# A hand-planned attention and FFN kernel on one core: the first FFN's gates freed from Wu in the plan, GpSimd's sums booked on the shared port, a longer lead for instruction loads, and the whole order planned anew

## The chip, the cores and the metric

One core of a Trainium2 chip. The metric is device time in microseconds (us) of one execution. The engines are called as the profile calls them: PE (TensorE, matrix products), PEld (its weight loads), ACT (ScalarE), DVE (VectorE), POOL (GpSimd), SP (SyncE, which here only issues DMAs).

## What is computed

Four layers over one sequence of 2048 rows of 512 bf16 values: attention with a memory, FFN, and both again with the same weights. Cut to what matters:

```python
x = x + A(layernorm(x));  x = x + B(layernorm(x))
x = x + A(layernorm(x));  x = x + B(layernorm(x))

def A(x):                       # 32 heads of 16; 4 segments of 512 rows
    for s in range(4):
        p = softmax(qs @ ks.T * 16**-0.5 + causal mask)
        a_dot = p @ vs
        a_mem = (phi(qs) @ M) / (phi(qs) @ z + 1e-6)   # phi(t) = t + 1 if t > 0 else exp(t)
        o = g * a_mem + (1 - g) * a_dot                # g = sigmoid(beta), one per head
        M = M + phi(ks).T @ vs;  z = z + phi(ks).sum()
    return o @ wo

def B(x):
    return (gelu(x @ w_gate) * (x @ w_up)) @ w_down    # 512 -> 1792 -> 512
```

## The kernel before, in words

The two attention layers have four segments each, so there are eight segments k = 0 to 7 of 512 rows, each with its attention `Att(k)` and its FFN `Ffn(k)`. For one segment: layer norm of four row tiles (VectorE's statistics, then xn, L920), transposed into xnT by DMA or by PE; q, k, v by products of 128x512; 36 rounds of scores, taken in pairs, whose exponentials ScalarE writes into `pt` (L1864); masks on `pt` by GpSimd (L1813, L1818) or VectorE (L1823); "flushes", which multiply `pt` with the values; transposes back on VectorE (L1391, L1414), and, for segments with a memory, the sum of both attentions into `aT` (L1417) on VectorE or GpSimd. Then come `wo` (added to x, L1463), the norm for the FFN, 14 gate tiles and 14 up tiles (wg_sb, wu_sb), gelu on ScalarE, their product on VectorE (L1557), and four down tiles of 14 products each (wd_sb). The update of the memory is a chain on VectorE: macc (L1303), zacc (L1305; L1301 in a first segment), mblk (L1286), zcols (L1292).

Nothing of the order is written down line by line. `order` is a list scheduler that runs when the kernel is built: it keeps a clock for each engine (`Clocks`, `Engine`), books each operation with a fixed duration, and emits instructions in the order that its clocks give. Each engine then runs its own list in order, and the semaphores that the tiles require hold it where data or a buffer isn't there yet. So the planner's durations and conditions decide only the order and, for some operations, the engine; the chip's waits come from the data.

What the change touches in it:

- `POLICY` and `STAGES`: some 60 constants (due times, slacks, preferences between engines), a set for each 20 us of planned time.
- `Clocks.issue`: a model of how PE's instructions come in, in chunks of 256. At place 178 of a chunk the planner notes that the next one is asked for; at place `CHUNK_END` it lets PE stand until `FETCH` us after that.
- [...] In `Engine.serve` a job with a `Port` waits in the plan until the other engine's port is free, less 0.2 us; `Port(t, True)` is the soft kind, beside which the other engine only pays 0.15 us.
- `on_dve_or_pool` posts a job to both engines, and the one that comes to it first takes it; `pol.at_pool` moves GpSimd's claim on the sums of `aT` earlier or later.
- The weights are loaded by SP (L600): 4 pieces of Wo, 8 of Wg, 8 of Wu in the list `pieces`, 7 of Wd in `late_pieces`, each with a planned time. The times of the first three are `w_at + 1.2 kt` and `w_at + 5 + w_gap n`, n = 0 to 7 for Wg and 8 to 15 for Wu. When the last of `pieces` is posted, the event ("loaded", "first") is set at the planner's estimate of its landing plus 2.0 us.
- `gate`: a gate of any FFN may be planned once its xnT is there and `free()` holds, which asks for ("loaded", "first"). `early` lets a gate begin with half of xnT. `up` asks only for its gelu.
- If PE would find nothing to do while scores remain, the planner gives it a filler product from the tile `warm`.

Nearly all products go through one helper line, L541, so the profile tells them apart by their tiles: "ps<-xnT,wg_sb" is a gate. Four products of 32 columns or rows of PE stand for one whole product; PE is then in its "columns" or "rows" mode, and the planner books 0.109 us for each change of mode.

Of the kernel before, what the change touches and what calls it, by code (L numbers as in the profile page):

```python
# [37 lines left out]
CHUNK, CHUNK_ASKED, CHUNK_END, FETCH = 256, 178, 222, 3.7  # L38
# [27 lines left out]
def table(halved):  # L66
# [17 lines left out]
    if halved:  # L84
# [31 lines left out]
    rs_pool=32.757, f_urge=-233.244, quick=2, paired=8, turn_pe=1, turn_last=0, w_at=29.345, w_gap=2.17,  # L116
    wd_at=78.552, wd_gap=2.776, flush_wait=-13.887, piece_slack=40.254, kb_slack=24.368, mem_slack=-20.134,
    margin=0.5, qk_due=0.962, e_q=49.408, e_k=2.993, exp_slack=-6.401, e_slack=131.01, phi_slack=22.785,
    gelu_slack=-0.789, act_evict=1.671, first_evict=0.248, gate_step=93.832, up_due=-100.529, up_step=84.355,
    down_due=-29.196, down_step=-47.297, upd_due=91.807, kb_act=82.777, vz_slack=55.93, x_dve=2.467, v0_due=-11.641,  # L120
    x1_at=-87.497, x2_at=16.051, x3_at=24.107, x3_load=-378.834, direct=2, gelu_tiles=0, look=3, lag=0.852,
    wv_at=-320.502, xn_pool=19.822, kb_pool=121.576, cut_pool=154.009, at_pool=-238.466, pe_turns=0, gate_due=4.191,
    shun=8.799, col_gap=0.807, hold=5, early=104.615, starve=0.16, near=114.234, cap=13, soon=28.208, columns=0,
    kd_slack=-5.85, zero_slack=-1.031, hold1=-49.923, hold2=2.205, hold3=11.541, hold_step=-162.485, hold_v=23.995,
    park=3)
# [3 lines left out]
        rs_pool=0.722, quick=9, kb_slack=2.193, mem_slack=-24.231, e_q=-2.643, gelu_slack=-0.49, gate_step=79.021,  # L129
        up_due=-101.483, up_step=41.973, down_step=-58.4, upd_due=91.729, vz_slack=33.291, direct=8, gelu_tiles=2,  # L130
        lag=0.412, at_pool=-237.424, early=83.209, starve=60.426, soon=7.146, park=4)),
    (2, 3, dict(
        rs_pool=2.667, quick=6, turn_pe=0, kb_slack=55.298, mem_slack=-32.756, e_q=-2.851, gelu_slack=-0.49,
        gate_step=78.038, up_due=-98.977, up_step=25.491, down_step=-53.827, upd_due=91.729, vz_slack=14.093,
        x_dve=7.459, direct=6, gelu_tiles=2, look=2.764, lag=0.475, xn_pool=30.206, cut_pool=102.189,
        at_pool=-237.424, gate_due=8.415, starve=1.292, soon=7.146, park=5)),
    (3, 4, dict(
        rs_pool=4.794, turn_pe=12, kb_slack=51.509, mem_slack=58.674, e_q=50.036, e_k=1.445, gelu_slack=1.935,
        gate_step=78.038, up_due=-96.513, up_step=85.14, down_step=-56.495, vz_slack=40.138, x_dve=6.187, direct=6,
        look=2.618, xn_pool=30.206, cut_pool=118.125, at_pool=-208.534, gate_due=14.291, shun=21.0, early=101.394,  # L140
        starve=0.321, soon=7.146, park=2)),
    (4, 5, dict(
        rs_pool=-2.341, quick=0, turn_pe=12, kb_slack=85.554, mem_slack=58.674, qk_due=1.009, e_q=50.137, e_k=1.464,
        gelu_slack=0.429, gate_step=79.294, up_due=-96.513, up_step=84.505, down_step=-72.139, vz_slack=51.333,
        x_dve=6.187, direct=3, gelu_tiles=2, xn_pool=20.238, cut_pool=148.746, at_pool=-208.534, gate_due=8.415,
        shun=21.0, early=101.394, starve=0.453, soon=7.146, park=2)),
    (5, 6, dict(
        rs_pool=36.794, quick=0, turn_pe=12, kb_slack=66.017, mem_slack=58.674, qk_due=1.009, e_q=55.15, e_k=2.984,
        gelu_slack=-0.805, gate_step=79.294, up_due=-96.513, down_step=-70.89, vz_slack=18.865, x_dve=7.455,
        gelu_tiles=2, look=2.835, lag=0.71, xn_pool=20.238, cut_pool=148.746, at_pool=-208.534, gate_due=0.276,  # L150
        shun=21.488, soon=7.146)),
    (6, 7, dict(
        rs_pool=11.417, f_urge=-261.392, quick=0, paired=11, turn_pe=0, flush_wait=0.581, piece_slack=36.524,
        kb_slack=76.591, mem_slack=-10.427, qk_due=-0.609, e_q=97.288, e_k=-5.757, exp_slack=-18.942, e_slack=69.536,
        phi_slack=30.587, gelu_slack=0.965, act_evict=1.166, gate_step=33.55, up_due=-80.509, down_due=-55.61,
        down_step=-81.567, upd_due=143.06, kb_act=60.08, vz_slack=4.039, x_dve=18.331, direct=0, gelu_tiles=2,
        look=2.622, lag=0.754, xn_pool=-3.088, kb_pool=116.679, cut_pool=153.155, at_pool=-189.709, gate_due=0.226,
        shun=85.539, hold=8, early=169.131, starve=0.31, near=101.522, cap=11, soon=0.694, kd_slack=37.99, park=6)),
    (7, 8, dict(
        rs_pool=-52.581, f_urge=-61.761, quick=3, paired=0, turn_pe=13, flush_wait=-3.039, piece_slack=92.516,  # L160
        kb_slack=220.906, mem_slack=57.517, qk_due=-30.647, e_q=-54.782, e_k=89.983, exp_slack=-17.861,
        e_slack=55.594, phi_slack=96.482, gelu_slack=214.751, act_evict=-149.173, gate_step=5.34, up_due=-0.69,
        up_step=3.923, down_due=12.354, down_step=-3.42, upd_due=-3.412, kb_act=75.691, vz_slack=-199.522,
        x_dve=3.843, direct=4, gelu_tiles=6, look=1.342, lag=0.004, xn_pool=-28.912, kb_pool=53.965, cut_pool=27.06,
        at_pool=-56.962, gate_due=-1.429, shun=104.852, hold=14, early=6.432, starve=57.777, near=-2.631, cap=0,
        soon=-55.855, kd_slack=-7.989, park=5)),
    (8, 9, dict(
        rs_pool=-52.581, f_urge=-145.617, quick=3, paired=0, turn_pe=9, flush_wait=-5.724, piece_slack=95.692,
        kb_slack=220.647, mem_slack=59.145, qk_due=-29.873, e_q=-54.782, e_k=89.76, exp_slack=-17.752,
        e_slack=55.641, phi_slack=95.445, gelu_slack=218.63, act_evict=-149.173, gate_step=5.34, up_due=-2.89,  # L170
        up_step=10.443, down_due=12.354, down_step=-3.42, upd_due=-3.412, kb_act=75.691, vz_slack=-188.382,
        x_dve=3.864, direct=5, gelu_tiles=6, lag=0.004, xn_pool=-26.431, kb_pool=53.965, cut_pool=27.06,
        at_pool=-56.962, gate_due=-1.429, shun=104.852, hold=14, early=6.432, starve=57.777, near=-2.631, cap=0,
        soon=-86.977, kd_slack=-7.989, park=5)),
    (9, 10, dict(
        rs_pool=-12.084, f_urge=-80.924, paired=7, turn_pe=0, flush_wait=-10.54, piece_slack=101.497,
# [396 lines left out]
def order(pol, nc, cst, seg, wrk, psp, A_x, A_wq, A_wk, A_wv, A_wo, A_beta, B_x, B_w_gate, B_w_up, B_w_down, out):  # L573
# [412 lines left out]
    class Att:  # L986
# [360 lines left out]
        def flush_item(self, flush, masked):  # L1347
# [30 lines left out]
            def done():  # L1378
# [42 lines left out]
                def turned(t):  # L1421
                    on_dve_or_pool(t, slack, pol.at_pool, Port(0.15 + 0.275 * part), Port(0.16 + 1.0 * part, True), add, there)
# [31 lines left out]
    class Ffn:  # L1454
        def __init__(self, k):
# [39 lines left out]
            def gate(ft):  # L1495
# [33 lines left out]
                def free():  # L1529
                    return ck.has(("loaded", "first")) and (k == 0 and ft >= HELD or (("down", k - 1) if k else ("upd", 0)) in ev)  # L1530
# [476 lines left out]
```

## Time and profile before

| | before |
|---|---|
| median of 3 runs | 538.3 us (537.09 to 540.27) |
| the profiled execution, own time | 536.81 us |
| its span, first to last instruction | 535.1 us |
| instructions | 24177 |
| ACT, DVE, POOL busy in the span | 445.9, 433.7, 268.1 us |
| DMA moved | 29.99 MB |
| granted clock of PE | 1.0 |

The profile's rows give, by group of instructions, busy time, the mean duration and the idle time before them with what ended it. A row of the timeline has the start, the duration, the engine, the line, the operation with its tiles and a count. A row of the waits has the one that waited, the one waited for, the sum in us, the number of times and the longest. A row of a table by stretches has, in this order, the busy times of PE, PEld, DVE, ACT and POOL, then PE's clock, the DMA share and GB/s. "issue" is time in which an engine waited for nothing that the profile shows.

### The profile page before, as it was taken

What the parts mean: (1) busy time and instruction counts of PE and PEld (TensorE: products, weight loads), DVE (VectorE), ACT (ScalarE), POOL (GpSimd) and SP (SyncE); (2) the same over time, 40 slices, a digit from 0 to 9 for tenths busy, and PEclk for the clock granted to TensorE, in tenths of its full rate; (3) what the DMA queues carried; (4) which work ended last, traced back from release to release, by engine and by line L of the source; (5) the groups of instructions that cost most, each with busy time, mean ns of one, the idle gap of its engine ahead of it and who ended that gap; (6) DMA issues with size and microseconds to landing.
All of it is one profiled execution on the core that took longest, in us unless ns stands there. A gap on an engine that the chain in (4) does not pass through costs nothing.

```text
span 535.1 us, 24177 instructions
## 1 busy us (share of the span) xinstructions
PE 525.1 (98%) x10697; PEld 276.3 (52%) x10697; DVE 433.7 (81%) x823; ACT 445.9 (83%) x598; POOL 268.1 (50%) x333
## 2 busy tenths in 40 slices
PE   9999989998999999999999999999999999999997
PEld 4454455444545454555564544555555456555554
DVE  6899996999997999879987788888977997586342
ACT  6999989887999989899898899799989988952320
POOL 2986472568541966528773366491654354500000
PEclk9999999999999999999999999999999999999999
DMA  8366940323231232201221113310260132102101
GB/s 268 76 121 139 215 141 4 69 41 73 44 60 24 49 55 42 33 12 25 51 44 31 25 24 32 61 34 1 52 103 3 33 51 52 24 2 51 33 2 41
DMA packets 76762, 29.99 MB, mean 56 GB/s; under 512 B 61042, under 2 KB 76658, under 8 KB 76658
## 3 DMA queue, kind: packets, MB, share of 16 engines
q1 hardware_dynamic: 76368, 28.20, 26.0%
q8 instruction: 83, 1.36, 1.0%
q10 hardware_dynamic: 290, 0.26, 0.1%
q14 instruction: 21, 0.17, 0.1%
HBM read 9.70 MB, written 2.10 MB: 22 GB/s over the span
## 4 chain that ended last, share of the span: by engine, by line
PE 77%; DVE 4%; ACT 3%; POOL 1%; issue 1%; DMA 0%; ACTq 0%
PE ps L541 77%; ACT pt L1864 1%; ACT gel_sb L1616 1%; POOL kx L726 1%; DVE xn L920 1%; ACT gel_sb L1519 1%; POOL e L1170 1%; ACT gel_sb L779 0%; DMA xnT<-xn 0%; DVE x_sb L1463 0%; DVE st L856 0%; DVE mblk L1286 0%; DVE byq L1391 0%; DVE x_sb L869 0%; ACT L1519 0%
## 5 line engine op out<-in xcount | busy, mean ns | idle before, releaser
L1864 ACT ACTIVATE pt<-ps 128x1024 bf16<-128x1024 f32 x288 | 278.9, 1036 | 26.8 <-PE ps L541 19.9
L1813 POOL TENSOR_SCALAR_AFFINE_SELECT pt<-pt 128x256 bf16<-128x256 bf16 (+1 forms) x192 | 113.6, 604 | 148.0 <-ACT pt L1864 145.6
L541 PE MATMUL ps<-xnT,wg_sb 128*32 128x512 bf16 (+3 forms) x1367 | 107.7, 362 | 0.3 <-DMA xnT<-xn 0.3
L541 PE MATMUL ps<-wd_sb,gel_sb 128*32 128x512 bf16 (+2 forms) x1431 | 106.1, 354 | 0.0
L541 PE MATMUL ps<-xnT,wu_sb 128*32 128x512 bf16 (+1 forms) x1252 | 103.6, 379 | 0.2 <-ACT gel_sb L1519 0.2
L1557 DVE TENSOR_TENSOR gel_sb<-gel_sb,ps 128x512 bf16<-128x512 bf16 x112 | 75.2, 683 | 30.8 <-PE ps L541 28.5
L541 PEld LDWEIGHTS <-gel_sb 128*32 128x32 bf16 (+1 forms) x1623 | 53.2, 97 | 41.2 <-issue 2.2
L541 PEld LDWEIGHTS <-wu_sb 128*32 128x32 bf16 (+1 forms) x1252 | 45.8, 97 | 45.3 <-issue 2.0
L541 PEld LDWEIGHTS <-wg_sb 128*32 128x32 bf16 (+1 forms) x1367 | 47.5, 97 | 38.7 <-issue 1.5
L1391 DVE STREAM_TRANSPOSE byq<-ps 128x512 f32<-128x512 f32 x64 | 45.4, 710 | 24.5 <-PE ps L541 23.8
L1170 POOL TENSOR_SCALAR e<-e 128x512 bf16<-128x512 bf16 x32 | 50.0, 1565 | 7.1 <-ACT e L1147 6.4
L1463 DVE TENSOR_TENSOR x_sb<-x_sb,ps 128x512 bf16<-128x512 bf16 (+1 forms) x54 | 34.0, 635 | 17.8 <-PE ps L541 17.7
L1818 POOL TENSOR_SCALAR_AFFINE_SELECT pt<-pt 64x1024 bf16<-64x1024 bf16 x32 | 38.1, 1192 | 17.8 <-ACT pt L1864 15.6
L541 PE MATMUL ps<-xnT,wk_sb 128*32 128x512 bf16 (+2 forms) x330 | 34.9, 377 | 0.7 <-ACT pt L1864 0.7
L541 PE MATMUL ps<-pt,vaug 128*32 128x256 bf16 (+2 forms) x1344 | 35.1, 239 | 0.1
L541 PE MATMUL ps<-wv_sb,xnT 128*32 128x512 bf16 (+1 forms) x227 | 32.4, 380 | 2.2 <-DVE x_sb L1463 1.8
L541 PE MATMUL ps<-xnT,wq_sb 128*32 128x512 bf16 (+2 forms) x339 | 34.0, 377 | 0.0
L1616 ACT ACTIVATE gel_sb<-gel_sb 128x1024 bf16<-128x1024 bf16 (+4 forms) x31 | 33.3, 1157 | 0.0
L541 PE MATMUL ps<-q,kx 32*128 32x64 bf16 (+2 forms) x1120 | 31.4, 217 | 0.6 <-ACT pt L1864 0.3
L541 PEld LDWEIGHTS <-vaug 128*32 128x32 bf16 x1344 | 27.2, 97 | 9.2 <-issue 1.6
L856 DVE BATCH_NORM_STATS2 st<-x_sb 128x6 f32<-128x512 bf16 x46 | 31.2, 679 | 0.4
L541 PEld LDWEIGHTS <-kx 32*128 32x128 bf16 x1120 | 16.8, 92 | 28.1 <-issue 27.4
(128 smaller groups left out, 722.1 us busy)
## 6 DMA issues: line engine op xcount, KB each, us to landing
vz<-vaug SPq DMA_DIRECT2D x14, 136.0 KB, 3.0
wg_sb<-in_B_w_gate_dram SPq DMA_DIRECT2D x8, 224.0 KB, 4.0
wu_sb<-in_B_w_up_dram SPq DMA_DIRECT2D x8, 224.0 KB, 3.9
wd_sb<-in_B_w_down_dram SPq DMA_DIRECT2D x7, 256.0 KB, 5.7
x_sb<-in_A_x_dram SPq DMA_DIRECT2D x3, 512.0 KB, 6.5
out_dram<-x_sb SPq DMA_DIRECT2D x12, 128.0 KB, 1.9
xnT<-xn SPq DMA_TRANSPOSE x56, 2.5
kx<-kf SPq DMA_DIRECT2D x12, 64.0 KB, 3.3
```

What stands on the lines that cost most here:

```text
L541: self.nc.tensor.matmul(*args, **kw)
L726: return lambda: eng.tensor_scalar(out=kx[:, :, C * which:C * which + n], in0=kf[:, :, 0:n], scalar1=masks[:, which:which + 1], scalar2=No ...
L856: nc.vector.bn_stats(out=self.st6[:, 0, :], in_=x_sb[:, self.tt0 + j, :])
L920: eng.tensor_scalar(out=xn[:], in0=x_sb[:, self.tt0 + j, :], scalar1=self.mv[:, j, 1:2] if self.wide else self.mv[:, j, 0:1], scalar2=self ...
L1170: lambda eng: eng.tensor_scalar(out=e[0][:], in0=e[0][:], scalar1=1.0, scalar2=None, op0=ALU.min), summed)
L1391: nc.vector.transpose(out=(self.byq[:, pars[0], :, :].rearrange("p a c -> p (a c)") if h is None else self.byq[:].rearrange("p u a c -> p ...
L1463: ck.dve.post(ck.made(), slack, (0.15 + 0.00104 * (c1 - c0), lambda: nc.vector.tensor_tensor(out=xt, in0=xt, in1=ps()[:, 0:c1 - c0], op=AL ...
L1557: ck.dve.post(ck.made(), NORMAL, (0.683, lambda: nc.vector.tensor_tensor(out=g, in0=g, in1=ps()[:], op=ALU.mult), lambda t: (ps.read(t), e ...
L1616: return (0.205 + 0.427 * (f1 - f0), lambda: nc.scalar.activation(out=g, in_=g, func=ACT.Gelu_apprx_tanh), lambda t: self.gelu_done(t, f0, ...
L1813: nc.gpsimd.affine_select(out=view, in_=view, pattern=[[0, 4], [0, n], [1, C]], compare_op=ALU.is_ge, fill=0.0, base=C, channel_multiplier=-1)
L1818: nc.gpsimd.affine_select(out=view, in_=view, pattern=[[0, 4 * TPS], [1, C]], compare_op=ALU.is_ge, fill=0.0, base=0, channel_multiplier=-1)
L1864: nc.scalar.activation(out=pt_all[:, s0:s0 + 2, 2 * p:2 * p + 2, :].rearrange("p r h c -> p h r c"), in_=ps_all[:, pair[0]:pair[1] + 1, :] ...
```

## The change

- Where the planner opens the gates: ("loaded", "gate"), set when the first 12 pieces (Wo and Wg) are posted and estimated in; the ups now ask for ("loaded", "first"), set by the other 8 (Wu). Both conditions stand for all FFNs, but only the first has them open.
- GpSimd's sum of `aT` is booked as holding the port (not soft), and VectorE's zacc as needing it.
- `CHUNK_END` 222 becomes 216, `FETCH` 3.7 becomes 4.2.
- All of `POLICY` that matters and almost all of `STAGES` is replaced. Among it: `w_at` 29.345 to 35.146, `w_gap` 2.17 to 1.684, `wd_at` 78.552 to 60.061, `wd_gap` 2.776 to 3.685. The code that computes is the same.

The diff, without the stages:

```diff
-CHUNK, CHUNK_ASKED, CHUNK_END, FETCH = 256, 178, 222, 3.7
+CHUNK, CHUNK_ASKED, CHUNK_END, FETCH = 256, 178, 216, 4.2
...
-    rs_pool=32.757, f_urge=-233.244, quick=2, paired=8, turn_pe=1, turn_last=0, w_at=29.345, w_gap=2.17,
-    wd_at=78.552, wd_gap=2.776, flush_wait=-13.887, piece_slack=40.254, kb_slack=24.368, mem_slack=-20.134,
...
+    rs_pool=0.342, f_urge=-239.247, quick=2, paired=12, turn_pe=5, turn_last=9, w_at=35.146, w_gap=1.684,
+    wd_at=60.061, wd_gap=3.685, flush_wait=3.556, piece_slack=44.291, kb_slack=75.413, mem_slack=21.416, margin=0.5,
...
-                             (0.154, lambda: nc.vector.tensor_tensor(out=zacc[:], in0=zacc[:], in1=self.zk[:],
+                             (Port(0.154), lambda: nc.vector.tensor_tensor(out=zacc[:], in0=zacc[:], in1=self.zk[:],
                                                                      op=ALU.add), kept)]
...
-                    on_dve_or_pool(t, slack, pol.at_pool, Port(0.15 + 0.275 * part), Port(0.16 + 1.0 * part, True), add, there)
+                    on_dve_or_pool(t, slack, pol.at_pool, Port(0.15 + 0.275 * part), Port(0.16 + 1.0 * part), add, there)
...
-                    return ck.has(("loaded", "first")) and (k == 0 and ft >= HELD or (("down", k - 1) if k else ("upd", 0)) in ev)
+                    return ck.has(("loaded", "gate")) and (k == 0 and ft >= HELD or (("down", k - 1) if k else ("upd", 0)) in ev)
...
-                return Item(lambda: k + pol.up_due + pol.up_step * place(ft), lambda: ck.has(("gel", k, ft), by=ck.pe + 0.6), dense(ps, pairs), done,
+                return Item(lambda: k + pol.up_due + pol.up_step * place(ft), lambda: ck.has(("loaded", "first")) and ck.has(("gel", k, ft), by=ck.pe + 0.6), dense(ps, pairs), done,
                             kind="up", ps=ps, after=("gel", k, ft))
...
-    left = {"first": len(pieces), "late": len(late_pieces)}
+    left = {"gate": 3 * KT, "first": 2 * KT, "late": len(late_pieces)}
...
-    for at, kb, piece in pieces:
-        ck.sp.post(at, pol.piece_slack, (0.59, piece, lambda t, kb=kb: landed("first", t, kb)))
+    for n, (at, kb, piece) in enumerate(pieces):
+        ck.sp.post(at, pol.piece_slack, (0.59, piece, lambda t, kb=kb, which="gate" if n < 3 * KT else "first": landed(which, t, kb)))
```

More of the change, by code (lines that the diff above doesn't have):

```diff
@@ L152 @@
-    (6, 7, dict(
[L153 to L158, printed above, removed]
@@ L159 @@
-    (7, 8, dict(
[L160 to L166, printed above, removed]
@@ L321 @@
[L321 to L327 removed]
+        hold=5, early=0.815, starve=0.325, near=178.081, cap=14, soon=101.079, kd_slack=62.624, park=4)),
```

352 lines of the change are left out of this document (188 added, 164 removed).

## The prediction

> **What bounds the kernel now.** I read the page's busy times first, then its chain, the long pieces of the chain, and the waits of TensorE (PE), longest first.
>
> ```profile
> PE 525.1 (98%) x10697; PEld 276.3 (52%) x10697; DVE 433.7 (81%) x823; ACT 445.9 (83%) x598; POOL 268.1 (50%) x333
> 356.06 175.83 PE ps L541 x3787
> PE ps L541 <- DVE x_sb L1463: 1.8, 1, 1.8
> PE ps L541 <- ACT pt L1864: 1.5, 5, 0.4
> PE ps L541 <- issue: 1.2, 2, 1.0
> PE ps L541 <- DVE warm L636: 1.1, 1, 1.1
> PE ps L541 <- DMA xnT<-xn: 0.3, 1, 0.3
> PE ps L541 <- ACT gel_sb L1519: 0.2, 1, 0.2
> ```
>
> The reader is to see that PE is the bound from the first microseconds to 531.89 (356.06 + 175.83), without a break in the last third. PE is idle for 535.1 - 525.1 = 10.0 us of the span. Of that, 535.1 - 531.9 = 3.2 are the last addition and store after the last product, and 1.1 the wait for the first memset; neither is touched. What an order can win back in waits is the other five rows: 1.8 + 1.5 + 1.2 + 0.3 + 0.2 = 5.0 us. Since PE never rests after 356, whatever PE saves before that arrives at the end in full, as long as no other engine becomes the bound.
>
> The multiplications themselves stay: every product of the reference is there before and after. So this change can bring little, and the question is which of those 5.0 us it removes, and what the new order adds.
>
> **The change part by part.** On the chip nothing of the first FFN's weights is waited for that wasn't before: each product has always waited by its own semaphores for its own tiles. All parts of the diff alter the written-out order of instructions and, for a few, the engine.
>
> *1. Gates without Wu.* Here is PE where the first FFN begins, then the two evictions that bring the first half of its input, then the weights.
>
> ```profile
> 68.89 0.33 PE L541 MATMUL ps<-warm 128*128 128x128 bf16 x3
> 69.30 0.22 PE L541 MATMUL ps<-warm 128*128 128x128 bf16 x1
> 70.50 0.55 PE L541 MATMUL ps<-warm 128*128 128x128 bf16 x7
> 73.06 1.92 PE L541 MATMUL ps<-xnT,wg_sb 128*32 128x512 bf16 x32
> 68.15 0.42 DVE L778 COPY xnT<-ps 128x512 bf16<-128x512 bf16 x1
> 68.47 0.58 ACT L779 ACTIVATE xnT<-ps 128x512 bf16<-128x512 bf16 x1
> L600 SPq DMA_DIRECT2D wg_sb<-in_B_w_gate_dram x8: 418/431/577, 34.5 to 54.0; - x8
> L600 SPq DMA_DIRECT2D wu_sb<-in_B_w_up_dram x8: 430/432/592, 54.5 to 64.3; - x8
> wg_sb<-in_B_w_gate_dram SPq DMA_DIRECT2D x8, 224.0 KB, 4.0
> wu_sb<-in_B_w_up_dram SPq DMA_DIRECT2D x8, 224.0 KB, 3.9
> 62.00:73.00 11.00, 10.56 (x197) 5.96 (x196) 10.66 (x26) 10.31 (x21) 6.45 (x6) 1.00 0.60 184
> 90.39 0.84 PE L541 MATMUL ps<-xnT,wu_sb 128*32 128x512 bf16 x12
> ```
>
> The products of "warm" are filler, put where the planner found nothing to do: 0.33 + 0.22 + 0.55 = 1.10 us busy with nothing, and in 62 to 73 another 11.00 - 10.56 = 0.44 idle. Wg was in at about 54.0 + 4.0 = 58, Wu only at 64.3 + 3.9 = 68.2, and the planner adds 2.0 to its own estimate of that, so in its books the first FFN was closed during just this hole. Half of xnT is there at 68.47 + 0.58 = 69.05, and half-width gates can run on it: the filler after 69.05 could be gates. I take 1.2 of the 1.10 + 0.44 = 1.54 us, leaving out what lies before 69.05; bounds 0 (other items were all it lacked, and gates wait for the second half of xnT) and 1.54. Much more is not there: gates cannot precede xnT, and xnT follows the last flush of segment 0, in a stretch where ScalarE (ACT) has little left to give, 10.31 of 11.00 in the same row.
>
> The wait is not removed but moved to the ups. Behind a waiting up on PE stands everything, since PE runs in order; but the ups began at 90.39, 22 us after Wu's landing. By the formula in the code the last Wg piece is posted at 35.1 + 5 + 7 x 1.684 = 51.9 where it was 29.3 + 5 + 7 x 2.17 = 49.5, the last Wu at 65.4 where it was 66.9. Cost nothing; the 15 us of slack of Wg and 22 of Wu hide it, and if they were gone each microsecond would be one of PE. The posts on SP are the same 4 + 8 + 8 + 7 at 0.43 us each; what passes them on SP (transposes of xn and the copies to kx) may wait behind a run of five, 2.2 us, as it did before. Zero, with 0.5 either way.
>
> *2. The longer lead for fetches.* The page gives the queue of instruction loads, and PE's timeline the place where PE waited for nothing else.
>
> ```profile
> q8 instruction: 83, 1.36, 1.0%
> 76.20 0.36 PE L541 MATMUL ps<-q,kf 16*128 16x192 bf16 x5 [0.99 <-issue]
> ```
>
> 83 loads of 1.36 MB / 83 = 16 KB feed 21394 products and weight loads, 258 each. The stop of 0.99 us lies in the middle of a group of score products, between two that need nothing new: a load that came late behind a burst of very short products. A plan that expects a load 0.5 us later puts longer products in front of it. I take 0.8 of the 1.2 us that "issue" holds; bounds 0 and 1.2. [...]
>
> *3. GpSimd's sums and the shared port.* VectorE (DVE) and GpSimd (POOL) ahead of PE's longest stop:
>
> ```profile
> 126.61 1.15 POOL L1417 TENSOR_TENSOR aT<-aT,amT 128x512 bf16<-128x512 bf16 x1 [0.31 <-DVE aT L1414]
> 126.62 1.29 DVE L920 TENSOR_SCALAR xn<-x_sb,mv,rs 128x512 bf16<-128x512 bf16 x1
> 127.72 2.53 POOL L1818 TENSOR_SCALAR_AFFINE_SELECT pt<-pt 64x1024 bf16<-64x1024 bf16 x2
> 127.83 1.09 DVE L1305 TENSOR_TENSOR zacc<-zacc,zk 128x4 f32<-128x4 f32 x1
> 128.84 0.40 DVE L920 TENSOR_SCALAR xn<-x_sb,mv,rs 128x512 bf16<-128x512 bf16 x1
> 131.44 1.46 PE L541 MATMUL ps<-wv_sb,xnT 128*128 128x512 bf16 x6 [1.82 <-DVE x_sb L1463]
> L1305 DVE TENSOR_TENSOR zacc<-zacc,zk x4: 115/156/1087, 127.8 to 408.2; 128x4 f32<-128x4 f32 x4
> 198.81 1.54 POOL L1170 TENSOR_SCALAR e<-e 128x512 bf16<-128x512 bf16 x1
> 198.89 0.99 DVE L920 TENSOR_SCALAR xn<-x_sb,mv,rs 128x512 bf16<-128x512 bf16 x2
> ```
>
> The same xn takes 1.29 us when it starts with POOL's sum, 0.40 two lines later: 0.89 lost. The tiny zacc, 0.156 as a median, takes 1.09 behind the mask: 0.93 lost. Together 1.82 us of delay on DVE, and the product at 131.44 stood 1.82 us for DVE's addition to x. Before, the planner booked the sum as costing a neighbour 0.15 and zacc as needing no port, which are the two edits. With both booked right, this stop can be planned around: I take all 1.8; bounds 0 and 1.8. If a sum moves to DVE instead, nothing is lost while DVE has room.
>
> The other GpSimd work stays booked as soft. The row at 198.89 shows two xn in 0.99 beside "e", some 0.09 each more than 0.40, so soft is right there. [...]
>
> *4. The order made anew.* Nearly every constant of the planner is replaced. The remaining waits, 1.5 + 0.3 + 0.2 = 2.0 us, are dealt anew. Changes of PE's tiling are paid in every order:
>
> ```profile
> 457.10 2.34 PE L541 MATMUL ps<-xnT,wg_sb 128*32 128x512 bf16 x40
> 459.38 0.29 PE L541 MATMUL ps<-q,kf 16*128 16x64 bf16 x8
> 500.58 2.77 PE L541 MATMUL ps<-xnT,wg_sb 128*32 128x512 bf16 x48
> 503.17 1.04 PE L541 MATMUL ps<-xnT,wu_sb 128*32 128x512 bf16 x16
> ```
>
> Without a change 48 quarter products take 503.17 - 500.58 = 2.59 us, 0.054 each; the 40 before 459.38 should take 2.16 and took 2.28, so a change costs about 0.12. Ten more or fewer of them are 1.2 us either way, unknown. New stops that no plan foresees: before had two of over 0.5 us (1.82 and 0.99). I charge half of one average of these, 0.7; bounds 0 and 2.8 (as many as before).
>
> Sum: -1.2 - 0.8 - 1.8 + 0.7 = -3.1 us. The profiled execution took 536.8 (span 535.1 and 1.7 around it), so 533.7 on its own time. The median of the three runs shown, 538.3, lies 1.5 above that execution, which would give 535.2. Single runs spread from 537.09 to 540.27; I forecast between the two, **534.4 us**.
>
> **The rivals.**
>
> *The larger gain.* All bounds at their good end: 1.54 + 1.2 + 1.8 = 4.5, and the other 2.0 us of waits gone as well: 536.8 - 6.5 = 530.3 on its own time, 531.0 as I place the median. For it: those waits are short and of one kind (0.4 at most for "ACT pt"). Against: a new order usually pays for one with another.
>
> *It does not do what it says.* The three stops go and as many come back elsewhere (+4.5 - 4.5): 537.5. For it: the stops at 76.2 and 131.44 came from durations that the plan did not know, and it still does not know all.
>
> *VectorE becomes the bound: slower.* These are the stretches where it has least room, beside a later one with plenty:
>
> ```profile
> 120.00:140.00 20.00, 17.97 (x429) 8.92 (x422) 19.19 (x37) 16.74 (x25) 16.14 (x19) 1.00 0.31 62
> 140.00:160.00 20.00, 19.78 (x314) 9.87 (x316) 19.22 (x35) 19.37 (x27) 9.36 (x12) 1.00 0.35 58
> 460.00:480.00 20.00, 20.00 (x441) 10.36 (x430) 14.00 (x22) 15.93 (x19) 4.91 (x6) 1.00 0.01 4
> ```
>
> The third column of busy times is DVE: 19.2 of 20 from 120 to 160, so 0.8 us of room in each 20. Starting the first FFN earlier draws its evictions and multiplications, and with them the second segment's, into this tight part; a sum kept off POOL comes on top. The price is that of 131.44: once DVE is behind by more than about 1 us where PE needs a bank back, PE stands 1.8. Three such stops beyond the present ones, with only parts 1 and 2 gained, give 536.8 + 5.5 - 2.0 = 540.3, or 541.8 as a median. It decides from DVE at over 19.7 of 20 in two neighbouring stretches. Against it: at present the one such stop comes from port delays, not from load alone.
>
> *Loads of instructions are not at fault* (part 2 is zero, the rest holds): 534.5 on its own time, 535.9 as a median: within 0.5%.
>
> **How the numbers follow.** About 0.5% (2.7 us) is what a measurement of this kernel can tell from no change: faster is below 535.6, slower above 541.0. The forecast has 0.44, of which 0.33 falls below 535.6 and 0.11 above; the larger gain 0.23; no net change 0.10; VectorE as the bound 0.19; the instruction loads 0.04. Faster: 0.33 + 0.23 = 0.56. Same: 0.11 + 0.10 + 0.04 = 0.25. Slower: 0.19. The range starts at 529.5, the larger gain with ten tiling changes fewer (531.0 - 1.2, rounded), and ends at 542.0, just past the slower rival; beyond lie about 0.1 on each side. The likeliest case's own range is 531.5 to 537.0.
>
> **What would show it.** Step 1: no "warm" products between 66 and 73, gates on PE by 70, ups still over 10 us after Wu's landing. Step 2: the "issue" wait of PE below 0.4 us. Step 3: no xn or zacc of over 1 us beside L1417 ahead of a PE stop, and no wait of PE for x_sb. The forecast is wrong if PE's idle time, start and end aside, is not clearly under 5.0 us, if DVE passes 19.7 in two stretches, or if PE's busy time changes by more than 2 us, which would mean that the new order pays or saves in tiling changes what I took as even.

## The result and the profile after

The changed kernel takes 540.03 us (median of 17 runs, 538.63 to 543.92); before takes 537.02 on the same chip (17 runs). The ratio is 1.0054, with a 95% interval of 1.0040 to 1.0069: **slower by 0.5%**, where I had forecast 0.7% faster. (The three runs of the table of before are the first of these 17; against 537.02 my 534.4 is 0.5% less.) The profiled execution took 540.29 (span 538.6).

The page's busy times of after, then what PE waited for (the one waited for, the sum in us, the number of times, the longest):

```profile
PE 527.7 (98%) x9908; PEld 272.7 (51%) x9908; DVE 435.3 (81%) x829; ACT 441.4 (82%) x607; POOL 273.9 (51%) x347
```

```profile
PE ps L553 <- DMA xnT<-xn: 1.6, 3, 0.8
PE ps L553 <- DVE warm L648: 1.1, 1, 1.1
PE ps L553 <- DVE x_sb L881: 1.1, 1, 1.1
PE ps L557 <- DVE xn L932: 1.0, 1, 1.0
PE ps L553 <- issue: 0.8, 1, 0.8
PE ps L553 <- ACT pt L1876: 0.8, 1, 0.8
```

PE idles 538.6 - 527.7 = 10.9 us instead of 10.0, and it is busy 2.6 us longer. The 1.8 us behind x_sb of L1463 are gone and the issue wait is 0.8 instead of 1.2, but other rows took their place. (Lines lie 12 lower than before: L553 was L541.)

To see where the time goes I lay the two traces beside each other by work. Each product of PE counts with the time that one of its shape takes on average in both traces; fillers and PE's transposes are left out, and a product that a trace lacks is put in by its weight load. **Lag** below is the time by which a kernel comes later than before to the same amount of work, each counted from its own first instruction and averaged over 4 us at the stated time of before. It is an estimate, good to some 0.5 us, since the orders differ. Two executions of one order can differ by more: after and a_gate, below, by 1.0 at the end. For after it is -0.9 at 60 us and **+2.1 at 80**. It falls by about 1 at 131, where before has its longest stop, stays near 1 up to 350, and rises by small steps to 2.2 at 490 and by 1.0 at 495, where the last FFN's input is transposed. It is 3.4 at the last product. So the one large step, 3.0 us, lies between 60 and 80 us; I call this stretch the hole. Here it is, PE's timeline of after (start, duration, count, and idle time ahead with what ended it); only fillers ("warm"), stops, wo and the first gates are shown:

```profile
63.33 0.29 PE L553 MATMUL ps<-pt,vz 128*32 128x64 bf16 x13 [0.81 <-issue]
...
64.76 0.33 PE L553 MATMUL ps<-warm 128*128 128x128 bf16 x3
...
65.46 3.87 PE L553 MATMUL ps<-wo_sb,aT 128*128 128x512 bf16 x16
69.60 0.24 PE L553 MATMUL ps<-warm 128*32 128x128 bf16 x4
...
70.90 0.29 PE L553 MATMUL ps<-warm 128*32 128x128 bf16 x8 [1.06 <-DVE x_sb L881]
...
71.70 0.46 PE L553 MATMUL ps<-warm 128*32 128x128 bf16 x20
72.95 0.40 PE L553 MATMUL ps<-q,kx 32*128 32x64 bf16 x8 [0.79 <-ACT pt L1876]
...
75.50 0.31 PE L553 MATMUL ps<-warm 128*128 128x128 bf16 x1
75.61 0.91 PE L553 MATMUL ps<-xnT,wg_sb 128*128 128x256 bf16 x4
```

The row of wo in before:

```profile
60.88 3.83 PE L541 MATMUL ps<-wo_sb,aT 128*128 128x512 bf16 x16
```

wo of segment 0, called wo(0) below, starts at 65.46, 4.6 us later. The first gate follows at 75.61 instead of 73.06. Between them PE has the norm's chain to wait for (x, its statistics, xn, xnT) and little else to do. The table of that stretch, before and then after (start:end, length, busy PE, PEld, DVE, ACT, POOL, PE's clock, DMA share, GB/s):

```profile
60.00:80.00 20.00, 18.52 (x372) 9.94 (x366) 18.76 (x39) 17.66 (x30) 12.35 (x13) 1.00 0.62 167
```

```profile
60.00:80.00 20.00, 17.22 (x468) 10.86 (x460) 17.25 (x38) 17.64 (x26) 13.63 (x19) 0.91 0.79 215
```

1.3 us less of PE, although more of it is fillers (0.33 + 0.24 + 0.29 + 0.46 + 0.31 = 1.63 us in the rows above, 1.10 in before's), and a mean clock of 0.91. Why wo comes late is read one stage earlier, on ScalarE. These are its last exponentials of segment 0 and the two of segment 1 that follow, before and then after (36 exponentials to a segment):

```profile
49.03 4.77 ACT L1864 ACTIVATE pt<-ps 128x1024 bf16<-128x1024 f32 x5
54.55 2.08 ACT L1864 ACTIVATE pt<-ps 128x1024 bf16<-128x1024 f32 x2
57.52 1.94 ACT L1864 ACTIVATE pt<-ps 128x1024 bf16<-128x1024 f32 x2
```

```profile
49.09 6.58 ACT L1876 ACTIVATE pt<-ps 128x1024 bf16<-128x1024 f32 x7
56.46 3.85 ACT L1876 ACTIVATE pt<-ps 128x1024 bf16<-128x1024 f32 x4
61.20 1.97 ACT L1876 ACTIVATE pt<-ps 128x1024 bf16<-128x1024 f32 x2
```

Segment 0's last exponential ends at 54.55 + 2.08 = 56.6 in before and at 56.46 + 3.85 = 60.3 in after. Its last flush, the transposes and wo can't begin without it.

### The profile page after: what moved, and what is told of

It reads as the page before. It is cut to its first block, busy times and chain, and to the rows that moved or that the text cites. A ratio compares the mean times of both kernels' runs of the same rounds, so it can differ in the third digit from the quotient of the medians.

```text
span 538.6 us, 22629 instructions
## 1 busy us (share of the span) xinstructions
PE 527.7 (98%) x9908; PEld 272.7 (51%) x9908; DVE 435.3 (81%) x829; ACT 441.4 (82%) x607; POOL 273.9 (51%) x347
## 4 chain that ended last, share of the span: by engine, by line
PE 81%; DVE 9%; ACT 5%; DMA 2%; issue 2%; POOL 1%; SPq 0%; ACTq 0%; DVEq 0%
PE ps L553 80%; ACT pt L1876 2%; DMA xnT<-xn 1%; DVE byq L1403 1%; DVE e L1163 1%; DVE x_sb L1475 1%; DVE ab L1419 1%; ACT gel_sb L1628 1%; DVE st L868 1%; ACT gel_sb L1531 1%; PE ps L557 1%; DVE x_sb L881 1%; DMA x_sb<-in_A_x_dram 1%; DVE aT L1426 1%; DVE gel_sb L1569 1%
## 5 line engine op out<-in xcount | busy, mean ns | idle before, releaser
L1825 POOL TENSOR_SCALAR_AFFINE_SELECT pt<-pt 128x256 bf16<-128x256 bf16 (+1 forms) x192 | 112.3, 599 | 149.0 <-ACT pt L1876 140.6
L553 PE MATMUL ps<-xnT,wg_sb 128*32 128x512 bf16 (+3 forms) x1007 | 106.7, 373 | 0.9 <-DMA xnT<-xn 0.8
L553 PE MATMUL ps<-wd_sb,gel_sb 128*32 128x512 bf16 (+3 forms) x1266 | 105.8, 362 | 0.0
L553 PE MATMUL ps<-xnT,wu_sb 128*32 128x512 bf16 (+1 forms) x955 | 104.5, 379 | 0.1
L553 PEld LDWEIGHTS <-gel_sb 128*32 128x32 bf16 (+1 forms) x1458 | 52.9, 97 | 41.3 <-issue 0.9
L553 PEld LDWEIGHTS <-wu_sb 128*32 128x32 bf16 (+1 forms) x955 | 43.5, 97 | 46.6 <-issue 1.6
L553 PEld LDWEIGHTS <-wg_sb 128*32 128x32 bf16 (+1 forms) x1007 | 44.5, 97 | 44.1 <-DMA xnT<-xn 1.6
L1182 POOL TENSOR_SCALAR e<-e 128x512 bf16<-128x512 bf16 x29 | 46.1, 1592 | 1.7 <-ACT e L1159 1.1
L1830 POOL TENSOR_SCALAR_AFFINE_SELECT pt<-pt 64x1024 bf16<-64x1024 bf16 x34 | 39.4, 1160 | 13.2 <-ACT pt L1876 12.1
L790 DVE CAST gel_sb<-ps 128x512 bf16<-128x512 f32 x45 | 30.1, 682 | 6.8 <-PE ps L553 6.4
L553 PE MATMUL ps<-xnT,wk_sb 128*32 128x512 bf16 (+2 forms) x270 | 35.3, 377 | 0.0
L553 PE MATMUL ps<-pt,vaug 128*32 128x256 bf16 (+2 forms) x1344 | 34.9, 239 | 0.1
L553 PE MATMUL ps<-xnT,wq_sb 128*32 128x512 bf16 (+2 forms) x270 | 34.5, 377 | 0.2
L1628 ACT ACTIVATE gel_sb<-gel_sb 128x512 bf16<-128x512 bf16 (+2 forms) x53 | 34.4, 732 | 0.0
L553 PEld LDWEIGHTS <-vaug 128*32 128x32 bf16 x1344 | 27.3, 97 | 10.9 <-issue 3.2
L553 PE MATMUL ps<-wv_sb,xnT 128*32 128x512 bf16 (+1 forms) x275 | 31.8, 380 | 0.8 <-DMA xnT<-xn 0.8
L553 PE MATMUL ps<-q,kx 32*128 32x64 bf16 (+2 forms) x1120 | 31.1, 217 | 0.9 <-ACT pt L1876 0.8
```

The source lines that it names most:

```text
L553: self.nc.tensor.matmul(*args, **kw)
L790: ck.dve.post(ck.made(), slack, (0.673, lambda: nc.vector.tensor_copy(out=dst(), in_=src()), end), taken=taken)
L1182: lambda eng: eng.tensor_scalar(out=e[0][:], in0=e[0][:], scalar1=1.0, scalar2=None, op0=ALU.min), summed)
L1628: return (0.205 + 0.427 * (f1 - f0), lambda: nc.scalar.activation(out=g, in_=g, func=ACT.Gelu_apprx_tanh), lambda t: self.gelu_done(t, f0, ...
L1825: nc.gpsimd.affine_select(out=view, in_=view, pattern=[[0, 4], [0, n], [1, C]], compare_op=ALU.is_ge, fill=0.0, base=C, channel_multiplier=-1)
L1830: nc.gpsimd.affine_select(out=view, in_=view, pattern=[[0, 4 * TPS], [1, C]], compare_op=ALU.is_ge, fill=0.0, base=0, channel_multiplier=-1)
```

## The experiments

The theory that came out of this comparison, called "late scores" in the later expectations: in the first 60 us the new order puts projections ahead of scores and gives ScalarE more to copy, so segment 0's exponentials end some 4 us later; by the time wo(0) comes, PE has used up the work that could have covered the norm behind it. The rivals: the freed gates, the extra transposes at the end, the bookings, and the clock.

### The parts of the change by themselves

**a_gate**: after, with the gates held by both Wg and Wu again.

```diff
-                    return ck.has(("loaded", "gate")) and (k == 0 and ft >= HELD or ...
+                    return ck.has(("loaded", "first")) and (k == 0 and ft >= HELD or ...
```

> The changed kernel with one condition put back: gates ask again for all of Wo, Wg and Wu. Theory: the gates of the first FFN are held by xnT and not by any weight, so the planner writes the same order, and this run repeats the changed kernel: 1.005 of before, within 0.002. Rival (the freed wait is worth something, 1.2 us as predicted): 1 to 2 us slower than the changed kernel, 1.007 to 1.009.

540.26 us, ratio to before 1.0057 (1.0026 to 1.0088). The order is instruction for instruction that of after: in the new order xnT comes later than Wu, and the condition that was freed holds nothing. That is the title edit of the change, and it is worth nothing here.

**b_gate**: the opposite, before with that edit alone.

```diff
-    left = {"first": len(pieces), "late": len(late_pieces)}
+    left = {"gate": 3 * KT, "first": 2 * KT, "late": len(late_pieces)}
...
-                    return ck.has(("loaded", "first")) and (k == 0 and ft >= HELD or ...
+                    return ck.has(("loaded", "gate")) and (k == 0 and ft >= HELD or ...
```

> The kernel before with the edit of the gates alone (they wait for Wo and Wg only, the ups for Wu); constants, bookings and fetches as before. Step 1 of the prediction: the gates that start at 73.06 us start by 71.2 and PE gains 1.2 us by 76 us. Rival, xnT was all that held them: the gates start within 0.3 us of 73.06, or start earlier on half of xnT and wait for the other half, and the gain by work at 76 to 80 us is under 0.4. The total says nothing: behind this point the order is made anew with constants chosen for another start, and 540 to 560 would not surprise either.

```profile
70.38 0.44 PE L541 MATMUL ps<-warm 128*128 128x128 bf16 x5
70.97 1.02 PE L541 MATMUL ps<-xnT,wg_sb 128*128 128x512 bf16 x4
```

The gates start at 70.97 instead of 73.06, and the lag goes from -0.1 at 63 us to -1.3 at 80: 1.2 us gained. Step 1 was right in its mechanism and its size, for the order of before. Behind it, this order falls apart: it gives 553.18, one run, with the lag +5.9 at 141 us. Is that the price of early gates, or of constants that were chosen for another course?

**b_gate2**: b_gate with the planner's constants from 80 us on chosen anew.

```diff
(stages from 4 on: other constants; the first 80 us, and all other lines, as in b_gate)
```

> The kernel before with the edit of the gates alone, as in b_gate, and the planner's constants from 80 us of planned time on chosen anew for it; the first 80 us are those of b_gate. Theory: what b_gate lost (553.2 us) is lost because the later constants were chosen for another course, not because freed gates harm. Then this kernel keeps the gain of step 1 at 77 us (lag -0.5 or better), has no jump of several us at 134 us, and takes 535 to 540 us. Whether the 1.2 us of step 1 show in the total depends on how good the new later stages are: at best 535.8, a ratio of 0.998. Rival: early gates take something from the second segment that no later order gives back (ScalarE's or VectorE's time between 77 and 134): then the lag still jumps by several us there and the total stays over 543.

539.93 us (12 runs), ratio 1.0050 (1.0028 to 1.0072). The lag is -0.9 at 80 us and -1.7 at 167, without a jump at 134: early gates take nothing from the second segment. Between 167 and 210 us this plan loses 4.6 us in stretches of its own, and the lag is 4.3 at the end. So the rival falls, and the later order decides the total. That step 1 is worth its 1.2 us in a total is not shown by any run.

**b_model**: before's constants with all edits of the code.

```diff
-    rs_pool=0.342, f_urge=-239.247, ...
+    rs_pool=32.757, f_urge=-233.244, ...
(POLICY and STAGES of before; all other lines as in after)
```

> The code edits of the change alone (the gates' and ups' conditions, both port edits, the fetch constants) with all planner constants of before. Theory (each set of constants is fitted to one set of durations, and the least edit scatters the order from then on): clearly slower than both kernels, 1.012 or more, with filler on PE. Rival (the truer durations help by themselves, as predicted): 0.993 to 1.000.

546.67 us, ratio 1.0147 (1.0107 to 1.0187). At 77 us it leads by 1.1, then it loses step by step (lag +2.0 at 149, +7.1 at 350, +10.6 at the end). So the code's edits alone don't gain. The likely reason, which b_gate2 supports, is that a shift in the early plan sends the later part another way, for which the constants weren't chosen.

**b_sum1**: before, with the one sum at 126.6 us on VectorE instead of GpSimd, the order otherwise as it was.

```diff
-... Port(0.16 + 1.0 * part, True), add, there)
+... Port(0.16 + 1.0 * part, True), (lambda eng: add(nc.vector)) if (k, b) == (1, 3) else add, there)
```

> The kernel before with one single sum of aT, the one that GpSimd does at 126.6 us beside VectorE's xn, done by VectorE; all else the same. Port theory of the prediction (that sum and the mask behind it put VectorE 1.8 us behind, and PE stands for it at 131.4): VectorE's xn falls back to 0.4, the wait of PE for x_sb of 1.8 us goes, and the kernel gains 1 to 1.8 us, 0.9967 to 0.998 of before. Rival (VectorE's own 0.6 us for the sum and the masks still meet it there): the wait stays over 1 us, 0.999 to 1.001.

```profile
126.19 0.43 DVE L1417 TENSOR_TENSOR aT<-aT,amT 128x512 bf16<-128x512 bf16 x1
126.73 0.41 DVE L920 TENSOR_SCALAR xn<-x_sb,mv,rs 128x512 bf16<-128x512 bf16 x1
127.06 0.15 DVE L1305 TENSOR_TENSOR zacc<-zacc,zk 128x4 f32<-128x4 f32 x1
...
129.70 1.46 PE L541 MATMUL ps<-wv_sb,xnT 128*128 128x512 bf16 x6 [0.42 <-DVE x_sb L1463]
```

xn 0.41 instead of 1.29, zacc 0.15 instead of 1.09, PE's stop 0.42 instead of 1.82. The lag goes from -0.4 at 121 us to -1.4 at 149 and is still -1.4 at the last product: 1.0 us gained. The median says 537.52, ratio 0.9987 (0.9959 to 1.0014): 1 us can't be told from nothing in it.

### Where the loss is not

**a_turn0**: after, without the transposes on PE that it adds for the last FFN's input.

```diff
-... turn_pe=5, turn_last=9, ...
+... turn_pe=5, turn_last=0, ...
```

> The changed kernel with the last FFN's input transposed by DMA, as before, in place of 16 products on PE (0.85 us of PE at 494.8 to 495.7 in the changed kernel's profile). If these products are plain added work at the end: 0.8 us less, 1.004 of before. Rival (the DMA transposes would be waited for there, since the last norm now ends later against the last downs): the same or slower, 1.005 to 1.008.

540.33, ratio 1.0062 (1.0041 to 1.0083). PE now waits 1.33 us for that input at 500.93 instead of spending 0.91 us on 16 transposes (494.82 to 495.73). So the transposes as such aren't the cause, but the place costs either way: the lag rises there by 1.0 in after (2.2 at 490 us, 3.2 at 500) and by 1.4 in a_turn0 (2.2 and 3.6). In the new order that input comes late.

**a_wide**: after, with fillers four times as wide, to see whether the fillers and the clock behind them are the loss.

```diff
-                product(ps()[:, 0:P], warm[:], wide[:, 0, :])
+                product(ps()[:], warm[:], wide)
```

> The changed kernel with its 21 filler products made 512 columns wide instead of 128, which is what the planner books for them; the order is the same. It is for the half clock of 72.75 to 76.25 us in the changed kernel's profile. Clock theory (most of the loss of 3 us is work done at half clock after the hole): the clock stays at 1.0 and the time falls by 1.5 to 2.5 us, to 1.001 to 1.003 of before. Rival (the hole itself costs, and while it lasts PE waits anyway): at most 0.6 us less, 1.004 to 1.006.

540.33, ratio 1.0055 (1.0020 to 1.0090). All seven executions kept a mean clock of 0.999 or 1.0, yet the median is no lower than that of after, and the lag of the profiled one, the fastest of the seven, is still 1.2 at 80 us (after: 2.1). So the clock isn't what makes the hole; at most 0.9 us of it.

### The price of late exponentials

**b_act6**: before, with six copies of 128x512 added on ScalarE among segment 0's exponentials (extra work, no result uses it).

```diff
+                if p == 0 and rounds[0] in [(0, 4), (0, 8), (0, 14), (0, 18), (0, 24), (0, 28)]:
+                    nc.scalar.activation(out=junk..., in_=wide, func=ACT.Copy)
```

> The kernel before with six added copies of 128x512 on ScalarE (writing a scratch tile; the output is untouched) among the exponentials of segment 0, so that ScalarE carries there what the changed order gave it. The order of the rest is that of before. Theory (ScalarE sets the pace from 10 to 62 us, PE has nothing else to do once the early projections are used up): the exponentials of segment 0 end 3.8 us later, the first gates start 2.5 to 4 us later, and the end comes 2 to 4 us later, 1.004 to 1.007 of before. Rival (PE has enough other work, so that ScalarE's delay is absorbed): under 1 us, below 1.002.

```profile
57.27 2.05 ACT L1864 ACTIVATE pt<-ps 128x1024 bf16<-128x1024 f32 x2
...
63.63 3.76 PE L541 MATMUL ps<-wo_sb,aT 128*128 128x512 bf16 x16
...
75.76 1.92 PE L541 MATMUL ps<-xnT,wg_sb 128*32 128x512 bf16 x32
```

Exponentials, wo and gates are 2.7, 2.75 and 2.7 us later than in before, the lag is 2.7 at 55 us and 3.5 at the end, and the time is 539.83, ratio 1.0053 (1.0037 to 1.0068), that of after. ScalarE's busy time is 3.3 us longer (449.2 instead of 445.9). So in this stretch some 3 us more of ScalarE cost some 3 us of the kernel. How much each order gives ScalarE to copy there is read from its groups between 10 and 58 us, before and then after:

```profile
L779 ACT ACTIVATE kf<-ps 128x512 bf16<-128x512 f32 x4 | 2.7, 666 | 0.0
L779 ACT ACTIVATE q<-ps 128x512 bf16<-128x512 f32 x4 | 2.5, 622 | 0.0
L779 ACT ACTIVATE vaug<-ps 128x512 bf16<-128x512 f32 x3 | 1.8, 632 | 0.0
```

```profile
L791 ACT ACTIVATE q<-ps 128x512 bf16<-128x512 f32 x6 | 4.2, 703 | 0.0
L791 ACT ACTIVATE vaug<-ps 128x512 bf16<-128x512 f32 x6 | 3.7, 732 | 0.0
L791 ACT ACTIVATE kf<-ps 128x512 bf16<-128x512 f32 x5 | 3.6, 716 | 0.0
```

17 evictions of q, k and v instead of 11, 11.5 us instead of 7.0: 4.5 us more on an engine that is busy for 47.19 of these 48 us in before and for 47.48 in after.

**a_dve6**: after, with six of these evictions on VectorE, PE's order kept.

```diff
+        def copy():
+            seen.append(1)
+            if len(seen) - 1 in (11, 19, 20, 23, 24, 25):
+                nc.vector.tensor_copy(out=dst(), in_=src())
+            else: nc.scalar.activation(out=dst(), in_=src(), func=ACT.Copy)
```

> The changed kernel with six of the PSUM reads that ScalarE does before segment 0's scores are done (all between 24 and 57 us) done by VectorE; order and everything else as in the changed kernel. ScalarE theory (its 100% from 20 to 60 us sets when the first FFN starts): segment 0's exponentials end 3 to 4 us earlier, the first gates start 2 to 4 us earlier, and the kernel gains 1.5 to 3 us on the changed one: 1.000 to 1.003 of before. Rival (the later part of the new order is what costs): the first gates come earlier, the end does not: 1.004 to 1.006. Second rival (VectorE has no room either): nothing moves, or it gets worse.

540.96, ratio 1.0063 (1.0043 to 1.0083), and wo(0) at 65.78. ScalarE now stands idle for 2.4 us ahead of exponentials, 1.9 of it for PE: the scores come late in PE's own order, because the plan thought ScalarE busy. That was a miss for "ScalarE alone". Taking the load away without changing the order gives nothing back; so the late scores are a matter of PE's order, and ScalarE's load alone doesn't explain them. **b_dve3**, before with three such evictions on VectorE, says the same from the other side.

> The kernel before with three of ScalarE's PSUM reads in segment 0 (near 23, 38 and 54 us, where VectorE has gaps) done by VectorE. ScalarE theory: three times 0.65 us off the engine that sets the pace, so 1 to 2 us off the end, 0.996 to 0.998 of before. Rival (VectorE, at 4.6 to 4.9 of 5 us in most of this stretch, becomes the one waited for): 0.999 to 1.003.

536.68, ratio 0.9984 (0.9960 to 1.0008): no difference that can be told. The last exponential of segment 0 ends at 56.5, as in before, and ScalarE idles 1.5 us instead of 0.5 ahead of the exponentials, 1.3 of it for PE.

### The order of the first 60 us

**a_early**: after, with three of the planner's constants set back to before's in the first three stages, up to 60 us.

```diff
(stages 0, 1, 2; all later stages and all other lines as in after)
-    e_k=0.601 / 4.702 / 6.286,  shun=0.39 / 0.4 / 6.924,  lag=0.362 / 0.626 / 0.558
+    e_k=2.993,                  shun=8.799,                lag=0.852 / 0.412 / 0.475
```

> The kernel after, with three of the planner's constants (e_k, shun, lag) set back to those of before for the first 60 us of planned time; nothing else. Theory, late scores: the loss of the change arises because its order of the first 60 us brings the last exponentials of segment 0 at 59.6 us instead of 55.4, so that wo(0) and the first FFN come late and PE runs out of work. With these three constants the exponentials end by 56.5, wo(0) begins by 62 (after: 65.5), the first gates by 72.5 (after: 75.6), and the lag behind the kernel before, counted by useful work of PE, is under 0.8 us at 80 us (after: 2.6). Rival, the hole is made by what the new order does after 60 us (gates, loads, GpSimd's bookings): wo(0) may be early, but the gates still begin near 75 and the lag at 80 stays over 2. Both expect the whole to be longer than after, 550 to 570, since the constants from 60 us on were chosen for another start; the total decides nothing.

```profile
55.45 1.94 ACT L1712 ACTIVATE pt<-ps 128x1024 bf16<-128x1024 f32 x2 [0.25 <-PE ps L389]
...
61.26 3.80 PE L389 MATMUL ps<-wo_sb,aT 128*128 128x512 bf16 x16
...
69.22 0.60 PE L389 MATMUL ps<-xnT,wg_sb 128*128 128x256 bf16 x4 [0.18 <-DMA wu_sb<-in_B_w_up_dram]
```

The exponentials end at 57.4 (11 evictions of q, k and v on ScalarE, as in before), wo starts at 61.26, the gates at 69.22, 6.4 us earlier than in after (their 0.18 us of waiting is put down to a DMA by its time; a gate doesn't read wu_sb). The lag at 80 us is **-3.0** where after has +2.1: 5.1 us between two kernels that differ only in three constants of the first 60 us. The gates also start before those of before (73.06); the freed condition probably has a part in it, but no run takes it out here. The total, 559.2 (one run), decides nothing, as foreseen: the lag rises from -1.4 at 110 us to 10.2 at 132, under later constants that were chosen for another start.

**b_v0**: before, with one constant changed to after's in the first 60 us, and nothing else of the change.

```diff
-    v0_due=-11.641
+    v0_due=2.368
```

> The kernel before, with one constant (v0_due, the due time of segment 0's value products) at the value of after for the first 60 us; code and all else as before. Theory, late scores: this alone brings the last exponentials of segment 0 at about 59, wo(0) at 63 to 65, the first gates at 75 to 76, and with them the hole between 62 and 77 us and a lag over 2 us at 80, though neither the new bookings nor the new load times nor the freed gates are in it. Rival, the hole is made by the bookings, loads or freed gates: no hole, a lag under 1 us at 80. Both expect the total above before, by 3 to 10 us, since the later constants were chosen for another start.

```profile
58.34 1.94 ACT L1712 ACTIVATE pt<-ps 128x1024 bf16<-128x1024 f32 x2 [0.23 <-PE ps L389]
...
63.27 3.63 PE L389 MATMUL ps<-wo_sb,aT 128*128 128x512 bf16 x15
...
72.94 0.63 PE L389 MATMUL ps<-warm 128*32 128x128 bf16 x16
76.05 2.77 PE L389 MATMUL ps<-xnT,wg_sb 128*32 128x512 bf16 x48
```

The hole is back, without any of the new bookings, load times or freed gates: the exponentials end at 60.3 as in after, wo starts at 63.27, fillers follow, the gates start at 76.05, and the lag goes from -1.4 at 62 us to +1.4 at 80, a step of 2.8. I had expected over 2 at 80, so the value is a miss; the step is about as large as in after (3.0), from a better start. The total is 543.58 (one run).

So the late scores are shown from both sides as the cause of the hole: putting them back removes it, and making them late brings it. What isn't shown is a kernel that has the early start and a good remainder, so by how much such a one would beat before stays open. That a difference in the hole reaches the end within after's own order is seen in three executions, one of each kernel: a_wide, after and a_gate, whose orders are the same but for the width of fillers, have lags of 1.2, 2.1 and 2.8 at 80 us and of 1.8, 3.4 and 4.4 at the end.

## Why the prediction was wrong, step by step

**Step 1 (gates without Wu, -1.2).** The working read the fillers at 68.9 to 71 in before rightly: b_gate wins 1.2 us there. But it took the place for granted in the new order. There xnT itself is late (gates at 75.61), Wu was posted by 68.2, and the freed wait is worth 0, as a_gate shows. Of the signs that I had named, no "warm" products and gates on PE by 70 failed; the ups begin at 91.06, still far behind Wu.

**Step 2 (lead for fetches, -0.8).** The issue row went from 1.2 to 0.8, so -0.4. The new stop, 0.81 at 63.33, sits in a burst of short products as the old one, 0.99 at 76.20, did, and just ahead of wo. The sign "below 0.4" failed. No run has this edit alone; b_model, where it meets before's constants, has 0.4 in the issue row, in another order. That such stops are late loads, which I had only argued, the packets of the instruction queue bear out: PE went on 1.30 us after a load's packet ended in before (74.90 and 76.20) and 1.35 us after it in after (61.98 and 63.33). The only other stop of over 0.15 us that these two traces put down to "issue", 0.21 at 124.24 in before, ended 1.39 us after one (122.85).

**Step 3 (port and sums, -1.8).** `Port` is the planner's booking for what it keeps apart on VectorE and GpSimd; that a port is what the two share is not shown by any run. The delays that the step counts are: with the sum on VectorE, b_sum1 has 0.41 for xn instead of 1.29 and 0.15 for zacc instead of 1.09. In after, too, the sum near 127.8 is on VectorE, and the xn and the zacc behind it take 0.40 and 0.15:

```profile
127.81 0.54 DVE L1429 TENSOR_TENSOR aT<-aT,amT 128x512 bf16<-128x512 bf16 x1
128.47 0.40 DVE L932 TENSOR_SCALAR xn<-x_sb,mv,rs 128x512 bf16<-128x512 bf16 x1
128.79 0.15 DVE L1317 TENSOR_TENSOR zacc<-zacc,zk 128x4 f32<-128x4 f32 x1
```

Its size was too large: b_sum1 takes 1.4 us off the stop, since PE still waits 0.42 us there, and 1.0 of it arrives at the end. I counted the whole stop as a gain.

**Step 4 (the new order, +0.7): the step that failed.** I charged a new order with half of one average unforeseen stop and bounded that by 2.8, "as many as before". With the other steps at what was measured, 0 - 0.4 - 1.0, the measured difference of 540.03 - 537.02 = 3.0 us leaves +4.4 for the new order. 3.0 of it is the hole alone: not stops between neighbours, but work placed in the wrong stage, so that PE had nothing left when it had to wait. Before's own profile spoke for it. From the end of wo(0), at 60.88 + 3.83 = 64.7, to the first gate at 73.06 lie 8.4 us of a chain that doesn't end on PE, and the 1.54 us of fillers and idle time in it can be read as a cover that was just used up: whatever came later at its head had to be paid. And its head hangs on ScalarE's exponentials: I had even written that ScalarE had little left to give, 10.31 of 11.00, but used it only as a bound for step 1. The remainder of step 4 is a balance of gains and losses elsewhere. After was 0.9 us ahead at 60 us, and between 350 us and the end it loses another 2.5. 1.0 of that is the late input of the last FFN; the cause of the small steps before it stays open, since PE isn't idle there in either kernel.

Two of the signs by which I had called the forecast wrong came true. PE's idle time without its start and end is 10.9 - 3.3 - 1.1 = 6.5 us, not under 5.0. And PE is busy 2.6 us longer, but hardly by the tiling changes that I had named: 16 more transposes make 0.9, and 3.4 us at half the clock (last section) can make up to 1.7. The times that I gave the cases as medians lie 0.7 to 1.5 us above their own times, by no one rule; over 17 runs the median of before is only 0.2 above its profiled execution.

**The rivals.** The slower one had the right sign for the wrong engine: VectorE has more room than before where I feared for it (the third busy time, 18.28 and 16.90 instead of 19.19 and 19.22).

```profile
120.00:140.00 20.00, 19.11 (x466) 9.90 (x462) 18.28 (x41) 16.42 (x27) 15.70 (x20) 1.00 0.37 66
140.00:160.00 20.00, 19.86 (x365) 10.01 (x361) 16.90 (x29) 20.00 (x27) 12.58 (x15) 1.00 0.37 55
```

In the hole it was ScalarE's exponentials that came late. The tiling changes, which I had left at "even", are nearly even: counted in the traces' products, 294 before and 298 after, so 0.5 us at 0.12 each. "Does not do what it says" came nearest in kind: about as many stops came as went, and the hole came on top.

## What to carry to other kernels

When an order is made anew, the cost isn't the average stop: find the stage in which a second engine is full (here ScalarE up to about segment 0's last exponential, busy for 47.19 us in before and 47.48 in after of the 48 from 10 to 58) and ask whether the new order gives that engine more work or feeds it later, since what is lost there can be paid in full by the chain behind it (b_act6: 3.3 us more of ScalarE, a lag of 3.5 at the end), while taking work off it without a new order won nothing (a_dve6, b_dve3). A freed wait was worth something only where it was the last to end (1.2 us in b_gate, nothing in a_gate), so ask for the new order too which wait ends last. And a plan whose constants were fitted to one course is no sum of its edits: edits and constants taken apart cost 7 to 22 us against before here (b_v0, b_model, b_gate, a_early; three of them one run each), and the small gains that some of them did bring showed only in the trace, stage by stage.

## What the runs showed of the hardware that I had not expected

**The clock.** In the profiled after, PE's granted clock falls to half for some 3.4 us in the hole (start:end, length, busy PE, clock, DMA share, GB/s):

```profile
72.00:72.50 0.50, 0.16 (x12) 1.00 0.31 36
72.50:73.00 0.50, 0.04 (x5) 0.81 1.05 241
73.00:73.50 0.50, 0.50 (x12) 0.50 1.07 352
...
76.00:76.50 0.50, 0.50 (x7) 0.78 1.07 348
```

8 of 17 runs of after have such a fall (mean clock 0.996 or 0.997), with a median of 540.45 against 540.02 for the other 9. Of the 61 runs of before beside the various kernels, 8 have one (mean clock 0.993 to 0.997), with a median of 540.35 against 537.12. So such a fall goes with 3.2 us in before and with 0.4 in after. Half the rate for 3.4 us can cost 1.7 us at most, so in before something else must go along with it, and what that is isn't shown; nor is the place of the fall in before, whose profiled execution has none. In that execution 1.82 us without a product (129.6 to 131.4) left the clock at 1.00. In after two stops of 1.06 and 0.79 us, with fillers between them, stood ahead of the fall, and PE was busy for 1.80 of the 3.40 us from 69.30 to 72.70. The profiled b_v0 has a fall of about the same length: its mean clock is 0.99 from 69 to 70 us, 0.50 from 70 to 73 and 0.80 from 73 to 74, so 0.02 + 3.00 + 0.40 = 3.42 us at half; PE was busy for 0.12 of the 1.00 us from 69 to 70. So the longest stop alone doesn't tell in which trace the clock falls. What sets a fall off, and why one execution of an order has it and another hasn't, isn't shown.

**GpSimd beside VectorE.** It wasn't only GpSimd's sum beside which VectorE's xn was slow: in b_sum1, with the sum away, the xn that ran beside the mask took 1.32 us, where the one before it took 0.41, and in after three xn took 2.76 us together (from 33.91) while two such masks ran (34.12 to 36.52). Not every one was slow: the xn at 128.84 in before, while two masks ran (127.72 to 130.25), took 0.40. I had left all of GpSimd's other work booked as soft because of one row; that was too broad.

```profile
127.13 1.32 DVE L920 TENSOR_SCALAR xn<-x_sb,mv,rs 128x512 bf16<-128x512 bf16 x1
127.17 2.89 POOL L1818 TENSOR_SCALAR_AFFINE_SELECT pt<-pt 64x1024 bf16<-64x1024 bf16 x2 [1.23 <-ACT pt L1864]
```
